# The 1e-9 of batch 0's softmax sums, added on GpSimd as separate pieces in a re-searched order

## The chip, the cores and the metric

The kernel runs on one core of a Trainium2 chip. The metric is the device time of one execution in microseconds (us), as the median of several runs; 699.75 us before the change (three runs, 699.62 to 700.32).

## The reference

Eight batches of slot attention with eight heads feed one feed-forward layer. Only what is computed matters here:

```python
a = np.exp(phi - np.max(phi, axis=2, keepdims=True))
a = a / (np.sum(a, axis=2, keepdims=True) + 1e-09)
k_m = np.einsum('bhsm,bhsd->bhmd', a, k)
v_m = np.einsum('bhsm,bhsd->bhmd', a, v)
scores = scale * np.matmul(q, k_m.transpose(0, 1, 3, 2))
attn = np.exp(scores - np.max(scores, axis=-1, keepdims=True))
attn = attn / (np.sum(attn, axis=-1, keepdims=True) + 1e-09)
attn_out = np.matmul(attn, v_m)
...
h = x @ w_in
g = 0.5 * h * (1.0 + erf(h * inv_sqrt2))
return g @ w_out
```

There are 576 positions per batch, 32 slots, heads of 64, a model width of 512 and a hidden width of 2048. x holds attn_out with the heads side by side. The 1e-9 that the title speaks of is the one in the second softmax, over the 32 slots.

## The kernel before, in words

The slot matrix v_m is multiplied into w_in (pieces `Up`, matmuls that write `pu`), so that hidden products run straight from the softmax weights: `h` = (p_hi, p_lo) times U. U and the weights p are each split into a high and a low part and go through three matmul passes; the same holds for g and w_out (`p`, 12 matmuls of 512 columns per block of 128 hidden units, with `gh`, `gl`, `wo_hi`, `wo_lo`). The weights arrive as 64-bit numbers and are decoded on the chip, one block of 128 hidden units at a time: two ScalarE instructions (`dB`, lines 309 and 310), three VectorE ones (`dC` 314, `dG` 318, `dS` 322) and an integer add on GpSimd (`dDi`, `dDo`, line 342); `dE` and `dF` split w_out. Sixteen such blocks exist for w_in and for w_out; the first eight serve batch 0 and batch 1 before the other eight are needed.

Batch 0 is treated apart, since nothing can run before its softmax. Its 576 positions are handled in three parts x = 0, 1, 2 (256, 256 and 64 positions). For each part the scores are transposed so that positions lie on partitions (`n_score`, writes `psc`), then VectorE takes the maximum (`n_max`, line 680) and subtracts it (`n_sub`, 685), ScalarE takes the exponential (`n_exp`, 692), VectorE sums over the slots (`n_sum`, 695), adds 1e-9 and takes the reciprocal (`n_inv`, 699 and 700), and multiplies (`n_mul`, also line 685). TensorE transposes back (`n_T`, writes `pT`, line 720), ScalarE and VectorE split the result into p_hi and p_lo (`n_hi` 735, `n_lo` 739). The sums are tiles `smx` of 128 partitions by 16, 16 and 8 numbers. The first hidden product (`h.0.0.0`, line 901) needs parts 0 and 1, the second half (`h.0.0.1`) needs parts 1 and 2.

All of this is written out as a list of some thousand pieces, `START`: a piece is a name with its arguments, as `n_inv.0` or `gelu.0.3.1`, and after a colon the engine where there is a choice (`a` ScalarE, `d` VectorE). `do` calls the function of each piece in the order of the list, and at the end every instruction is pinned behind the one before it on its engine. Each engine thus runs its own instructions in the list's order, and DMAs are issued from SyncE's queue in that order too. From batch 3 on, a plan by steps takes over where the list ends.

The hidden products alternate between two PSUM buffers (tag `h`, two of them): `h.0.1.1` writes the buffer that `gelu.0.0.1` (lines 921 and 922) has to have read. The pu products and the scores of later batches share one PSUM pair (tag `at`). One SBUF buffer serves phi of every batch, so phi of batch 1 is loaded once batch 0's transposes (line 457) have read it.

Of the kernel before, what the change touches and what calls it, by code (L numbers as in the profile page):

```python
# [64 lines left out]
at.1.1.4 at.1.0.4 dG.2.0 n_T.2 atc.1.1.4 atc.1.0.4:a n_hi.2 slots.1.0 dC.3.1 dDi.2 anorm.1
Lkv.1.1.3 n_lo.1 Lkv.1.1.4 n_lo.2 h.0.0.1 gelu.0.0.0 Lphi.2.0 dS.3.1 km.1.0 dG.3.1 Lwo.4
Up.0.2.1 gelu.0.0.1 Lwi.5 dF.2 dB.3.0 dDo.3 h.0.1.0 Lwo.7 Uh.0.2:d Lwo.5 Ul.0.2 h.0.1.1
gh.0.0:a Lphi.2.1 dC.3.0 Lwi.7 slots.1.1 gelu.0.1.1 gl.0.0 Lwi.6 gelu.0.1.0 dG.3.0 dE.3
h.0.2.0 km.1.1 dS.3.0 gh.0.1:a amax.2.0 dDi.3 dB.4.0 slotsT.1 h.0.2.1 kT.1:d dF.3 dB.4.1
Up.0.3.1 dC.4.0 dG.4.0 p.0.0 Uh.0.3 dB.5.0 gl.0.1 Ul.0.3 gelu.0.2.1 dG.5.0 gelu.0.2.0 dB.5.1  # L70
dC.4.1 dS.4.0 score.1.0 dC.5.0 dDi.4 h.0.3.0 Lq.1.1 sT.1.0.1 sT.1.0.0 Lwo.6 h.0.3.1 dS.5.0
dG.4.1 dDi.5 Up.0.4.1 gelu.0.3.1 max.1.0 p.0.1 Uh.0.4:a gelu.0.3.0 Ul.0.4 sub.1.0 dS.4.1
dC.5.1 exp.1.0 dDo.4 gh.0.2:a sum.1.0 Up.0.5.1 dG.5.1 h.0.4.0 Uh.0.5:a dE.4 gl.0.2 h.0.4.1
gh.0.3:a Ul.0.5 dS.5.1 p.0.2 dF.4 dDo.5 inv.1.0 gelu.0.4.1 amax.2.1 dB.6.0 dC.6.0 mul.1.0
gelu.0.4.0 dE.5 score.1.1 gl.0.3 dB.6.1 h.0.5.0 dS.6.0 dF.5 p.0.3 gh.0.4:a dG.6.0 dB.7.1
dC.6.1 dDi.6 pT.1.0 gelu.0.5.0 sT.1.1.1 dB.7.0 sT.1.1.0 dS.6.1 h.0.5.1 gl.0.4 dG.6.1 Up.0.6.1
gelu.0.5.1 gh.0.5:a dC.7.0 p.0.4 dDo.6 Uh.0.6 Ul.0.6 max.1.1 Lwi.9 sub.1.1 aexp.2.1 Lwo.8
Lwi.8 dG.7.0 exp.1.1 Up.1.0.4 Lwo.9 dC.7.1 dE.6:a gl.0.5 h.0.6.0 Uh.1.0 dS.7.0 p.0.5 dG.7.1
dDi.7 aexp.2.0 Ul.1.0 ph.1.0:a dS.7.1 dF.6 dDo.7 sum.1.1 gelu.0.6.0 Up.0.7.1 h.0.6.1 Uh.0.7:a
Ul.0.7 inv.1.1 h.0.7.0 gelu.0.6.1 dE.7:a gh.0.6:d h.0.7.1 gl.0.6 gelu.0.7.0 dB.8.1 p.0.6  # L80
pl.1.0 Lwo.10 dF.7 Lphi.3.1 gelu.0.7.1 Lwi.10 gh.0.7:a mul.1.1 dB.8.0 gl.0.7 dC.8.0 p.0.7
dB.9.0 pT.1.1 dG.8.1 dB.9.1 ph.1.1:d pl.1.1 o.0.2.7:a dC.9.0 h.1.0.0 dC.8.1 dS.9.0 h.1.0.1
dG.9.1 gelu.1.0.0 h.1.1.0 dC.9.1 gelu.1.0.1 dG.8.0 o.0.0.7:a h.1.1.1 dS.8.1 gh.1.0:a o.0.3.7:a
gl.1.0 Up.1.4.4 o.0.1.7:a dS.8.0 gelu.1.1.0 p.1.0 dG.9.0 dDi.8 gelu.1.1.1 Uh.1.4:a gh.1.1:a
Ul.1.4 dDo.8 h.1.2.0 dE.8:d Lwo.11 h.1.2.1 dF.8 Lq.2.0 gelu.1.2.0 Lwi.11 gl.1.1 h.1.3.0
gelu.1.2.1 gh.1.2:d h.1.3.1 gl.1.2 gelu.1.3.0 dB.10.1 p.1.1 Lwo.12 gelu.1.3.1 dG.10.1 dB.10.0
dC.10.1 dS.9.1 dC.10.0 dDo.9 dG.10.0 h.1.4.0 h.1.4.1 gelu.1.4.0 dDi.9 h.1.5.0 gelu.1.4.1
dE.9:a p.1.2 dF.9 Lwo.13 Lwi.13 gh.1.3:d dB.11.0 dS.10.1 Lwi.12 gl.1.3 dDo.10 gelu.1.5.0
gh.1.4:d h.1.5.1 dB.11.1 p.1.3 dE.10:d gelu.1.5.1 dS.10.0 amax.3.1 dDi.10 gl.1.4 h.1.6.0
dG.11.1 p.1.4 dC.11.1 gelu.1.6.0 gh.1.5:a gl.1.5 dF.10 dC.11.0 h.1.6.1 dS.11.0 dG.11.0 p.1.5  # L90
gelu.1.6.1 dS.11.1 dDi.11 dB.12.0 dB.12.1 dDo.11 h.1.7.0 dG.12.1 Lwi.14 dE.11:a mw.2 gh.1.6:a
Up.0.8.4 gl.1.6 h.1.7.1 Uh.0.8:a dF.11 p.1.6 dC.12.1 gelu.1.7.0 dG.12.0 gelu.1.7.1 gh.1.7:a
dS.12.1 dB.13.0 dDo.12 gl.1.7 p.1.7 dB.13.1 Ul.0.8 dC.12.0 dS.12.0 aexp.3.1 o.1.2.7:d dDi.12
h.0.8.0 dC.13.1 h.0.8.1 Lwi.15 gelu.0.8.0 dG.13.1 o.1.3.7:a Lphi.3.0 Up.1.8.4 gelu.0.8.1
dC.13.0 mr.2 o.1.1.7:d gh.0.8:a Lwo.15 h.0.9.0 o.1.0.7:d Lwo.14 h.0.9.1 dE.12:d gelu.0.9.0
dF.12 Uh.1.8:a h.0.10.0 dS.13.1 gl.0.8 dDo.13 p.0.8 Ul.1.8 dE.13:a gelu.0.9.1 dF.13 gh.0.9:a
h.0.10.1 dB.14.0 gl.0.9 p.0.9 dG.13.0 gelu.0.10.0 dS.13.0 gelu.0.10.1 gh.0.10:a dDi.13 gl.0.10
dB.15.0 h.0.11.0 dG.14.0 Up.0.12.2 dC.14.0 h.0.11.1 dC.15.0 Uh.0.12:a amax.3.0 dB.15.1 p.0.10
dG.15.0 mw.3 Lphin.2 dS.14.0 gelu.0.11.1 Ul.0.12 gelu.0.11.0 dDi.14 gh.0.11:a gl.0.11 h.0.12.0
dS.15.0 h.0.12.1 dDi.15 p.0.11 gelu.0.12.1 gelu.0.12.0 dB.14.1 gh.0.12:a Up.0.14.2 h.0.13.0  # L100
Uh.0.14:a Ul.0.14 h.0.13.1 gelu.0.13.0 gl.0.12 h.0.14.0 gelu.0.13.1 dG.14.1 gh.0.13:a p.0.12
dC.14.1 gelu.0.14.0 dS.14.1 dC.15.1 dDo.14 anorm.2 gl.0.13 aexp.3.0 Lphi.4.1 h.0.14.1 Lphi.4.0
dS.15.1 dG.15.1 Lkv.2.0.0 h.0.15.0 Lkv.2.0.2 dE.14:d dDo.15 p.0.13 gelu.0.15.0 gelu.0.14.1
gh.0.14:a gl.0.14 dF.14 h.0.15.1 dE.15:d p.0.14 gelu.0.15.1 gh.0.15:d dF.15 gl.0.15 aadd.2
p.0.15 o.0.0.15 mr.3 Lkv.2.1.0 o.0.1.15 Lkv.2.1.4 amax.4.0 Lkv.2.0.3 h.1.8.0 o.0.3.15 o.0.2.15
h.1.8.1 Lkv.3.0.2 gelu.1.8.0 Lkv.2.0.1 Up.1.12.4 gelu.1.8.1 Lkv.2.1.1 gh.1.8:a Lkv.2.1.2
h.1.9.0 Lkv.2.0.4 Uh.1.12:d Lkv.2.1.3 h.1.9.1 gelu.1.9.0 os.0.1 gl.1.8 h.1.10.0 Ul.1.12 p.1.8
gelu.1.10.0 gelu.1.9.1 gh.1.9:d gl.1.9 aexp.4.0 ax.2 h.1.10.1 p.1.9 gelu.1.10.1 slots.2.0
slots.2.1 h.1.11.0 km.2.1 Lphin.3 gh.1.10:d gl.1.10 h.1.11.1 gelu.1.11.0 Lkv.3.1.4 km.2.0
os.0.3 p.1.10 gelu.1.11.1 Lkv.3.0.4 gh.1.11 gl.1.11 slotsT.2 kT.2:d h.1.12.0 score.2.0  # L110
gelu.1.12.0 h.1.12.1 sT.2.0.0 Lq.2.1 aadd.3 Lkv.3.0.1 p.1.11 gelu.1.12.1 gh.1.12:a gl.1.12
sT.2.0.1 max.2.0 ax.3 p.1.12 h.1.13.0 h.1.13.1 gelu.1.13.0 h.1.14.0 gelu.1.13.1 gh.1.13:d
h.1.14.1 gelu.1.14.0 gl.1.13 p.1.13 gelu.1.14.1 gh.1.14:a gl.1.14 sub.2.0 exp.2.0 h.1.15.0
sum.2.0 h.1.15.1 inv.2.0 p.1.14 gelu.1.15.0 mul.2.0 gelu.1.15.1 gh.1.15:a pT.2.0 gl.1.15
tg.1.0 p.1.15 ph.2.0:d pl.2.0 o.1.0.15 Up.2.0.4 Lkv.3.1.0 Lq.3.1 tp.1.0 Uh.2.0:a Lkv.3.0.0
Ul.2.0 o.1.2.15 h.2.0.0 o.1.3.15 h.2.1.0 tg.1.1 score.2.1 gelu.2.1.0 o.1.1.15 gelu.2.0.0
tp.1.1 Lq.3.0 sT.2.1.0 sT.2.1.1 Lkv.3.1.1 max.2.1 Lkv.3.1.3 Lkv.3.0.3 amax.4.1 Lkv.3.1.2
tg.1.2 os.1.1 Up.2.12.4 anorm.3 Up.2.4.4 tg.1.3 tp.1.2 Uh.2.4:a Ul.2.4 aexp.4.1 h.2.2.0
Lphi.5.0 Up.2.8.4 Lphi.5.1 mw.4 h.2.3.0 Uh.2.8:d tp.1.3 gelu.2.3.0 gelu.2.2.0 gh.2.0.0:d
Ul.2.8 sub.2.1 gl.2.0.0 slots.3.0 to.1 gh.2.0.1:d slots.3.1 gl.2.0.1 Lkv.4.0.3 exp.2.1 os.1.3  # L120
h.2.4.0 sum.2.1 Lkv.4.0.2 P.2.0.0 mr.4 inv.2.1 Lphin.4 gelu.2.4.0 mul.2.1 Lkv.4.0.1 pT.2.1
Lkv.4.0.4 h.2.5.0 h.2.6.0 gelu.2.5.0 P.2.0.1 gelu.2.6.0 gh.2.0.2:a Uh.2.12:a gl.2.0.2 km.3.1
h.2.7.0 P.2.0.2 gelu.2.7.0 gh.2.0.3:d gl.2.0.3 Ul.2.12 P.2.0.3 km.3.0 amax.5.0 amax.5.1 mw.5
Lkv.4.1.1 h.2.8.0 Lkv.4.1.2 Lkv.4.1.0 h.2.9.0 Lkv.4.1.4 gelu.2.8.0 Lkv.4.1.3 slotsT.3
Lkv.4.0.0 kT.3 h.2.10.0 gelu.2.9.0 gh.2.0.4:d score.3.1 gelu.2.10.0 score.3.0 h.2.11.0
sT.3.0.1 sT.3.0.0 h.2.12.0 max.3.0 gelu.2.11.0 gh.2.0.5:a h.2.13.0 gl.2.0.4 gl.2.0.5
gelu.2.12.0 P.2.0.4 sT.3.1.1 aadd.4 sT.3.1.0 h.2.14.0 P.2.0.5 gelu.2.14.0 gelu.2.13.0 gh.2.0.6
ph.2.1:d max.3.1 aexp.5.0 anorm.4 h.2.15.0 gl.2.0.6 ax.4 sub.3.0 P.2.0.6 pl.2.1 gelu.2.15.0
# [1146 lines left out]
```

## Time and profile before

| | us |
|---|---|
| median of three runs | 699.75 |
| lowest, highest | 699.62, 700.32 |
| the profiled execution's own time | 699.25 |
| its span, first to last instruction | 697.5 |
| TensorE busy (matmul) | 683.4 |
| VectorE busy | 374.5 |
| ScalarE busy | 306.9 |
| GpSimd busy | 45.9 |

The profiled execution is 0.50 us under the median. A matmul's end is modelled, so TensorE's busy time is not its time at full rate; what can be read from it is where TensorE was idle, and for whom it waited. The mean granted TensorE clock was 0.991. "PEq", "SPq" and the like are sequencers, which issue and wait.

### The profile page before, as it was taken

What the parts mean: (1) busy time and instruction counts of PE and PEld (TensorE: products, weight loads), DVE (VectorE), ACT (ScalarE), POOL (GpSimd) and SP (SyncE); (2) the same over time, 40 slices, a digit from 0 to 9 for tenths busy, and PEclk for the clock granted to TensorE, in tenths of its full rate; (3) what the DMA queues carried; (4) which work ended last, traced back from release to release, by engine and by line L of the source; (5) the groups of instructions that cost most, each with busy time, mean ns of one, the idle gap of its engine ahead of it and who ended that gap; (6) DMA issues with size and microseconds to landing.
All of it is one profiled execution on the core that took longest, in us unless ns stands there. A gap on an engine that the chain in (4) does not pass through costs nothing.

```text
span 697.5 us, 12343 instructions
## 1 busy us (share of the span) xinstructions
PE 683.4 (98%) x4942; PEld 568.3 (81%) x4942; DVE 374.5 (54%) x691; ACT 306.9 (44%) x787; POOL 45.9 (7%) x38
## 2 busy tenths in 40 slices
...
GB/s 328 367 298 103 125 189 138 43 154 173 27 222 141 84 208 1 66 193 134 162 1 57 57 2 31 1 99 1 30 1 31 84 1 31 1 31 0 31 1 46
DMA packets 30717, 64.37 MB, mean 92 GB/s; under 512 B 3780, under 2 KB 8644, under 8 KB 30660
## 3 DMA queue, kind: packets, MB, share of 16 engines
...
q10 hardware_dynamic: 96, 0.13, 0.1%
q14 instruction: 18, 0.15, 0.1%
...
## 4 chain that ended last, share of the span: by engine, by line
PE 91%; DMA 3%; DVE 2%; ACT 1%; issue 0%; SPq 0%; POOL 0%; POOLq 0%; ACTq 0%; DVEq 0%
PE acc L941 49%; PE h L901 28%; PE tacc L941 6%; PE pu L619 4%; DMA kv<-kv 1%; PE psc L619 1%; DMA w_in_sb<-w_out 1%; PE psc L536 1%; DMA raw<-w_in 1%; DMA phi<-phiT 1%; PE x L536 1%; DVE raw L318 0%; PE pk L536 0%; DVE wo_lo L348 0%; ACT aT L244 0%
## 5 line engine op out<-in xcount | busy, mean ns | idle before, releaser
L901 PE MATMUL h<-p_hi,U 128*128 128x288 f32 x1024 | 203.2, 297 | 0.0
L941 PE MATMUL acc<-wo_hi,gh 128*128 128x512 f32 x512 | 200.4, 391 | 0.0
L941 PE MATMUL acc<-wo_hi,gl 128*128 128x512 f32 x512 | 199.6, 390 | 0.0
L941 PE MATMUL acc<-wo_lo,gh 128*128 128x512 f32 x512 | 199.6, 390 | 0.0
L913 ACT ACTIVATE gf<-h 128x256 f32<-128x256 f32 x192 | 74.0, 387 | 254.8 <-issue 180.0
L901 PEld LDWEIGHTS h<-p_hi,U 128*128 128x128 f32 x1024 | 163.5, 188 | 22.0 <-issue 7.9
L244 DVE CAST gh<-gf 128x512 fp32r<-128x512 f32 x103 | 44.2, 429 | 175.8 <-ACT gf L913 169.2
L941 PEld LDWEIGHTS acc<-wo_hi,gl 128*128 128x128 f32 x512 | 96.1, 188 | 21.1 <-DVE gl L928 0.6
L941 PEld LDWEIGHTS acc<-wo_hi,gh 128*128 128x128 f32 x512 | 96.4, 188 | 20.4 <-DVE gl L928 3.4
L941 PEld LDWEIGHTS acc<-wo_lo,gh 128*128 128x128 f32 x512 | 96.1, 188 | 15.8
L901 PE MATMUL h<-p_lo,U 128*128 128x288 f32 x512 | 108.7, 294 | 0.0
L928 DVE TENSOR_TENSOR gl<-gf,gh 128x512 fp32r<-128x512 f32 x128 | 90.4, 707 | 20.0 <-ACT gh L244 10.9
L901 PEld LDWEIGHTS h<-p_lo,U 128*128 128x128 f32 x512 | 81.2, 188 | 0.4 <-DVE p_lo L739 0.4
L860 DVE TENSOR_TENSOR U<-pu,U 128x512 fp32r<-128x512 f32 (+2 forms) x50 | 40.9, 836 | 44.0 <-ACT U L244 43.9
L244 ACT CAST U<-pu 128x512 fp32r<-128x512 f32 (+2 forms) x47 | 32.0, 710 | 18.3 <-PE pu L619 13.5
L915 ACT ACTIVATE tails<-h 128x32 f32<-128x32 f32 x192 | 37.3, 194 | 0.0
L619 PE MATMUL pu<-w_in_sb,kT 64*32 64x512 f32 (+2 forms) x624 | 34.4, 528 | 1.3 <-POOL w_in_sb L342 0.8
L941 PE MATMUL tacc<-wo_hi,gh_t 128*128 128x512 f32 x64 | 25.4, 397 | 0.0
L941 PE MATMUL tacc<-wo_lo,gh_t 128*128 128x512 f32 x64 | 24.9, 390 | 0.0
L941 PE MATMUL tacc<-wo_hi,gl_t 128*128 128x512 f32 x64 | 24.9, 390 | 0.0
L919 ACT ACTIVATE gf<-h 128x288 f32<-128x288 f32 x32 | 13.2, 414 | 24.6 <-PE h L901 15.9
L342 POOL TENSOR_TENSOR y<-y,raw 128x512 int32<-128x512 int32 x14 | 20.5, 1462 | 47.4 <-DVE y L322 23.6
...
## 6 DMA issues: line engine op xcount, KB each, us to landing
...
```

The source lines that it names most:

```text
L244: return e.copy(dst, src) if e is nc.scalar else e.tensor_copy(dst, src)
L342: nc.gpsimd.tensor_tensor(w, y, low, op=ALU.add)
L536: nc.tensor.matmul(pk[32 * j : 32 * j + 32, : 2 * D], st["aT", b][:, c, g, 32 * j : 32 * j + 32], st["kv", b, g, c][:, :, j, :], start=(c ...
L619: nc.tensor.matmul(ps[g][M * j : M * j + M], st["kT", b][rows, t, M * j : M * j + M], moving[j][rows], start=True, stop=True,)
L860: nc.vector.tensor_sub(u[:, ..., 1, :], pu, u[:, ..., 0, :].bitcast(F32))
L901: i = nc.tensor.matmul(h[:, :HS], u[g][w], x[:, g, :], start=(n == 0), stop=(n == 3 * G - 1))
L913: nc.scalar.activation(gf[:, f % 2 * n : f % 2 * n + n], h[:, :n], AF.Gelu)
L915: nc.scalar.activation(t, h[:, n:HS], AF.Gelu)
L919: nc.scalar.activation(gf[:, :HS], h[:, :HS], AF.Gelu)
L928: nc.vector.tensor_tensor(g_of("gl", *k), g_of("gf", *k), g_of("gh", *k).bitcast(F32), op=ALU.subtract)
L941: nc.tensor.matmul(acc, x, w[:, f, :], start=(first and n == 0), stop=(last and n == 2))
```

## The change

A piece `n_eps` holds the addition of 1e-9 for batch 0's parts, on GpSimd; `n_inv` keeps the reciprocal on VectorE. The order is a new one: the same 1004 pieces and the three `n_eps`, in a list that differs from its first line, with another choice of engine in 37 of the pieces. The other batches' addition (line 790 before) is not touched.

```diff
@@ -694,9 +694,12 @@
     def n_sum(x):
         nc.vector.tensor_reduce(part0(x, "smx"), part0(x, "s"), axis=AX.X, op=ALU.add)
 
+    def n_eps(x):
+        m = part0(x, "smx")
+        nc.gpsimd.tensor_scalar_add(m, m, 1e-9)
+
     def n_inv(x):
         m = part0(x, "smx")
-        nc.vector.tensor_scalar_add(m, m, 1e-9)
         nc.vector.reciprocal(m, m)
...
-        "n_inv": n_inv, "n_mul": n_mul, ...
+        "n_eps": n_eps, "n_inv": n_inv, "n_mul": n_mul, ...
@@ -50,99 +50,99 @@
 START = """
-Lwo.1 Lphi.0.1 Lphi.0.0 Lkv0.0.0 Lkv0.1.0 Lwo.0 dB.1.1 Lq.0.0 amax.0.1 Lq.0.1 dC.1.1 aexp.0.1
...
+Lwo.1 Lphi.0.1 Lphi.0.0 Lkv0.0.0 Lkv0.1.0 Lwo.0 dB.1.1 Lq.0.0 amax.0.1 aexp.0.1 amax.0.0
...
```

On VectorE, the place is the softmax of batch 0's parts 0 and 1. `smx` are the sums, `s` the exponentials, `mx` the maxima; line 348 is `dF`, line 860 (863 after) splits U, lines 314, 318 and 322 decode weights, line 426 is batch 1's maximum of phi. Before:

```order
L318 TENSOR_SCALAR raw_147<-raw_147 128x512
L695 TENSOR_REDUCE smx_0_376<-s_0_303 128x16
L426 TENSOR_REDUCE nm_280<-phi_209 128x1
L695 TENSOR_REDUCE smx_1_385<-s_1_339 128x16
L699 TENSOR_SCALAR smx_0_376<-smx_0_376 128x16
L700 RECIPROCAL smx_0_376<-smx_0_376 128x16
L680 TENSOR_REDUCE mx_2_399<-psc_2_305 128x8
L685 TENSOR_TENSOR s_0_303<-s_0_303,smx_0_376 128x512
L348 TENSOR_TENSOR wo_lo<-y_246,wo_hi 128x512
L860 TENSOR_TENSOR U_0_411<-pu_0_402,U_0_411 128x2x128
L699 TENSOR_SCALAR smx_1_385<-smx_1_385 128x16
L700 RECIPROCAL smx_1_385<-smx_1_385 128x16
```

and after:

```order
L695 TENSOR_REDUCE smx_0_350<-s_0_299 128x16
L322 TENSOR_SCALAR y_246<-y_246 128x512
L318 TENSOR_SCALAR raw_147<-raw_147 128x512
L426 TENSOR_REDUCE nm_271<-phi_185 128x1
L695 TENSOR_REDUCE smx_1_391<-s_1_346 128x16
L703 RECIPROCAL smx_0_350<-smx_0_350 128x16
L348 TENSOR_TENSOR wo_lo<-y_246,wo_hi 128x512
L685 TENSOR_TENSOR s_0_299<-s_0_299,smx_0_350 128x512
L863 TENSOR_TENSOR U_0_407<-pu_0_398,U_0_407 128x2x128
L703 RECIPROCAL smx_1_391<-smx_1_391 128x16
L314 TENSOR_SCALAR y_412<-y_412 128x512
L685 TENSOR_TENSOR s_1_346<-s_1_346,smx_1_391 128x512
```

The two additions are gone from VectorE, the first sum has moved ahead of two decoding steps, and the third part's maximum (line 680) has moved behind both multiplications.

On GpSimd, the place is the same stretch; after the change its queue reads:

```order
L342 TENSOR_TENSOR y_246<-y_246,raw_147 128x512
L342 TENSOR_TENSOR w_in_sb<-y_149,raw_134 128x4x128
L699 TENSOR_SCALAR smx_0_350<-smx_0_350 128x16
L342 TENSOR_TENSOR w_in_sb<-y_246,raw_147 128x4x128
L699 TENSOR_SCALAR smx_1_391<-smx_1_391 128x16
L342 TENSOR_TENSOR y_412<-y_412,raw_314 128x512
L699 TENSOR_SCALAR smx_2_482<-smx_2_482 128x8
L342 TENSOR_TENSOR w_in_sb<-y_412,raw_314 128x4x128
```

Before, the same line-342 additions stood there in the same order with nothing between them; now one of the three small additions stands behind each of three of them.

On ScalarE, the place is the first hidden products of batch 0; `gf` is the gelu's output, `h_0` and `h_1` the halves, `km` batch 1's slots, lines 309 and 310 a weight's decoding. Before:

```order
L919 ACT_TABLE_LOAD
L919 ACTIVATE gf_0_547<-h_0_0_478 128x288
L579 ACTIVATE km_552<-pk_0_506,rz_530 128x2x64
L921 ACTIVATE gf_0_547<-h_1_0_540 128x224
L922 ACTIVATE tails<-h_1_0_540 128x64
L309 ACTIVATE y_396<-w_in_sb 128x512
L310 ACTIVATE w_in_sb<-w_in_sb 128x512
```

and after:

```order
L922 ACT_TABLE_LOAD
L922 ACTIVATE gf_0_547<-h_0_0_474 128x288
L579 ACTIVATE km_551<-pk_0_508,rz_485 128x2x64
L309 ACTIVATE y_469<-w_in_sb 128x512
L310 ACTIVATE w_in_sb<-w_in_sb 128x512
L924 ACTIVATE gf_0_547<-h_1_0_540 128x224
L925 ACTIVATE tails<-h_1_0_540 128x64
```

A pair of decoding instructions has moved ahead of the gelu of the second half.

## Rows read from the trace of the kernel before

**Rows 1.** Windows by stage: from:to and length, then busy us by engine, clock, DMA.

```profile
core 0: us, PE busy (x) PEld busy (x) DVE busy (x) ACT busy (x) POOL busy (x), PEclk, DMA share, GB/s
...
15.00:35.00 20.00, 15.66 (x228) 10.79 (x229) 19.70 (x49) 16.92 (x41) 6.69 (x5) 0.74 0.98 369
35.00:62.00 27.00, 26.56 (x268) 20.00 (x267) 25.12 (x50) 24.25 (x53) 10.11 (x7) 1.00 0.53 193
62.00:693.00 631.00, 631.00 (x4338) 529.41 (x4336) 324.88 (x582) 257.61 (x678) 27.10 (x19) 1.00 0.23 74
```

**Rows 2.** The waits of TensorE: us in total, times, longest us.

```profile
PE pk L561 <- DMA kv<-kv: 1.8, 2, 1.6
PE pT L720 <- DVE s L685: 1.0, 3, 0.5
...
PE pu L619 <- DVE sT L758: 0.2, 1, 0.2
...
PE pu L619 <- DVE kT L244: 0.2, 1, 0.2
```

**Rows 3.** Timeline of VectorE, 23 to 32 us: start us, us, instruction.

```profile
23.90 0.65 DVE L699 TENSOR_SCALAR smx<-smx 128x16 f32<-128x16 f32 x1
24.58 0.25 DVE L700 RECIPROCAL smx<-smx 128x16 f32<-128x16 f32 x1
...
26.56 0.16 DVE L699 TENSOR_SCALAR smx<-smx 128x16 f32<-128x16 f32 x1
26.76 0.25 DVE L700 RECIPROCAL smx<-smx 128x16 f32<-128x16 f32 x1
...
30.96 0.34 DVE L699 TENSOR_SCALAR smx<-smx 128x8 f32<-128x8 f32 x1
31.34 0.20 DVE L700 RECIPROCAL smx<-smx 128x8 f32<-128x8 f32 x1
```

**Rows 4.** Timeline of GpSimd, 0 to 36 us; in brackets the idle time ahead.

```profile
1.01 0.29 POOL masks.py:199 TENSOR_SCALAR_AFFINE_SELECT ident<-ident 128x128 f32<-128x128 f32 x1
...
21.76 2.75 POOL L342 TENSOR_TENSOR w_in_sb<-y,raw 128x512 int32<-128x512 int32 x2 [4.32 <-DVE y L322]
29.97 1.30 POOL L342 TENSOR_TENSOR y<-y,raw 128x512 int32<-128x512 int32 x1 [5.46 <-ACT p_hi L735]
```

**Rows 5.** Timeline of TensorE, 19 to 62 us.

```profile
24.59 0.68 PE L619 MATMUL pu<-w_in_sb,kT 64*32 64x128 f32 x16 [0.82 <-POOL w_in_sb L342]
...
28.70 1.76 PE L457 MATMUL pt<-ident,phi 128*128 128x128 f32 x8
30.22 0.52 PE L901 MATMUL h<-p_hi,U 128*128 128x288 f32 x2
...
32.22 0.44 PE L720 MATMUL pT<-ident,s 128*128 128x128 f32 x2 [0.18 <-DVE s L685]
...
36.30 0.69 PE L901 MATMUL h<-p_hi,U 128*128 128x288 f32 x4
```

**Rows 6.** Timeline of ScalarE, 19 to 39 us.

```profile
29.44 0.68 ACT L735 CAST p_hi<-pT 128x288 fp32r<-128x288 f32 x2
...
35.65 0.22 ACT L922 ACTIVATE tails<-h 128x64 f32<-128x64 f32 x1
35.76 0.68 ACT L309 ACTIVATE y<-w_in_sb 128x512 f32<-128x512 f32 x1
...
36.90 0.60 ACT L244 CAST gh<-gf 128x512 fp32r<-128x512 f32 x1
```

**Rows 7.** Timeline of SyncE's DMA issues, 4 to 20 us: start us, us.

```profile
5.01 1.06 SPq L406 DMA_DIRECT2D q<-q  x2
10.64 0.33 SPq L358 DMA_DIRECT2D phi<-phiT  x1
```

**Rows 8.** Windows around the stretch of low TensorE clock, columns as in Rows 1.

```profile
20.00:30.00 10.00, 8.18 (x130) 5.90 (x122) 9.90 (x25) 8.31 (x20) 2.78 (x3) 0.50 1.04 387
30.00:40.00 10.00, 9.54 (x136) 7.21 (x135) 8.81 (x25) 9.12 (x25) 4.88 (x4) 0.99 0.87 318
```

More of the change, by code (lines that the diff above doesn't have):

```diff
@@ L65 @@
[L65 to L128, printed above, removed]
-gh.2.0.7 gl.2.0.7 h.2.0.1 slots.4.0 gelu.2.0.1 slots.4.1 h.2.1.1 Lphin.5 P.2.0.7 gelu.2.1.1
-Lkv.5.0.0 gh.2.1.0 Lkv.5.0.1 gl.2.1.0 Lkv.5.0.2 Lkv.5.0.3 km.4.0 km.4.1 Lkv.5.0.4 O.2.0.0
@@ new lines @@
+Uh.0.1:a dB.2.0 n_max.2 n_T.1 Ul.0.1 Lwi.5 dS.2.1 at.1.1.0 Lkv.1.1.2 n_sub.2 n_hi.0 at.1.0.0
+dG.2.1 n_exp.2 dB.3.1 n_lo.0 h.0.0.0 dDo.2 n_sum.2 anorm.1 atc.1.1.0 dC.2.0 n_eps.2
+atc.1.0.0:a n_inv.2 n_hi.1 n_mul.2 at.1.1.4 at.1.0.4 dG.2.0 n_T.2 atc.1.1.4 atc.1.0.4:a n_hi.2
+slots.1.0 dS.2.0 dC.3.1 Lkv.1.1.3 dDi.2 n_lo.2 n_lo.1 Lkv.1.1.4 h.0.0.1 gelu.0.0.0 Lwi.4
+dS.3.1 km.1.0 dB.3.0 Lwo.4 Up.0.2.1 dG.3.1 Lphi.2.0 h.0.1.0 Lwo.5 dC.3.0 gelu.0.0.1 dDo.3
+Uh.0.2:d Lphi.2.1 dE.2:a h.0.1.1 Ul.0.2 Lwo.6 gh.0.0:a dS.3.0 Lwi.6 slots.1.1 gelu.0.1.1 dF.2
@@ new lines @@
+Lwi.7 gelu.0.1.0 Lwo.7 dE.3 dG.3.0 h.0.2.0 km.1.1 gl.0.0 dB.4.0 dDi.3 slotsT.1 h.0.2.1 kT.1:d
+gh.0.1:a dF.3 gelu.0.2.0 Up.0.3.1 dC.4.0 p.0.0 Uh.0.3 dG.4.0 dB.5.0 gl.0.1 dC.5.0 gelu.0.2.1
+Ul.0.3 dS.4.0 dG.5.0 dDi.4 gh.0.2:a score.1.0 amax.2.0 dB.5.1 h.0.3.0 sT.1.0.0 Lq.1.1 sT.1.0.1
+dC.5.1 dB.4.1 h.0.3.1 gl.0.2 Up.0.4.1 dS.5.0 dC.4.1 dDi.5 p.0.1 Uh.0.4:a max.1.0 Ul.0.4
+sub.1.0 dG.4.1 exp.1.0 dS.4.1 p.0.2 sum.1.0 dDo.4 amax.2.1 gelu.0.3.0 gelu.0.3.1 dG.5.1 dE.4
+dS.5.1 gh.0.3:a dF.4 dDo.5 Up.0.5.1 dB.6.0 h.0.4.0 Uh.0.5:d Ul.0.5 h.0.4.1 inv.1.0 dE.5 Lwo.8
@@ new lines @@
+dC.6.0 gl.0.3 dB.6.1 score.1.1 dG.6.0 p.0.3 gelu.0.4.1 dC.6.1 dF.5 mul.1.0 dB.7.1 dS.6.0
+pT.1.0 dDi.6 gelu.0.4.0 h.0.5.0 sT.1.1.0 gh.0.4:a sT.1.1.1 dB.7.0 h.0.5.1 dS.6.1 gl.0.4
+Up.0.6.1 gelu.0.5.1 dG.6.1 p.0.4 Uh.0.6 dC.7.1 gelu.0.5.0 dDo.6 max.1.1 gh.0.5:a Ul.0.6 dG.7.1
+Lwi.9 Lwi.8 gl.0.5 aexp.2.0 Lq.2.0 Up.1.0.4 dC.7.0 aexp.2.1 dG.7.0 p.0.5 dE.6:a Lphi.3.0
+sub.1.1 Uh.1.0 dS.7.0 exp.1.1 dDi.7 Ul.1.0 dF.6 h.0.6.0 dS.7.1 Up.0.7.1 gelu.0.6.0 sum.1.1
+dDo.7 h.0.6.1 Uh.0.7:a Ul.0.7 inv.1.1 h.0.7.0 gelu.0.6.1 ph.1.0:a gh.0.6:d h.0.7.1 gl.0.6
```

102 lines of the change are left out of this document (75 added, 27 removed).

## The prediction, made before the result

> **What bounds the kernel now.** I read the shares of busy time first, then the span cut into stages, then what TensorE waited for, and only then the timelines of the 30 us in which the changed pieces stand. TensorE is busy 683.4 of 697.5 us (the table), but that is an average over unlike stages. Cut up [rows 1], it says more: from 62 to 693 us TensorE is busy for all 631.0 us, so nothing that VectorE or GpSimd does there can make the kernel shorter; it can only add a stall. The last 4.5 us are the final eviction and its DMA, which the change does not touch. What can be gained lies in the first 62 us, where TensorE is idle for 20.00 - 15.66 = 4.3 us from 15 to 35 and for 27.00 - 26.56 = 0.4 from 35 to 62; before 15 us no changed instruction stands.
>
> From 15 to 35 us VectorE is busy for 19.70 of 20 us, ScalarE for 16.92, and the DMA engines' share is 0.98 [rows 1]. This is the stage in which the three additions stand, and VectorE is the fullest engine in it. But the time comes out at TensorE, so the waits decide [rows 2]: it waited for VectorE's softmax multiplications 1.0 us in three pieces, for VectorE's two later releases 0.2 and 0.2, for key and value loads 1.8. Those on VectorE add up to 1.4 us, which caps what a lighter VectorE can give by itself.
>
> **The change part by part.** The sum is made against the profiled execution (699.25 us; its span is 697.5, and 1.75 lie around it). The median of the runs is 0.5 us above it, and I add that at the end.
>
> *Three additions leave VectorE.* From the start of each to the start of the reciprocal behind it [rows 3]: 24.58 - 23.90 = 0.68, 26.76 - 26.56 = 0.20, 31.34 - 30.96 = 0.38, together 1.26 us. They differ although they do nearly the same work. The first ends at 24.55, when GpSimd's pair of decoding additions ends (21.76 + 2.75 = 24.51); the third ends at 31.30, when another ends (29.97 + 1.30 = 31.27) [rows 3, 4]; the second, with GpSimd idle, takes 0.16. So two of them stood still until GpSimd was done. An addition that nothing holds costs 0.20, three cost 0.60. The bounds of what VectorE is freed of are 0.60 (the holding falls on whatever VectorE runs next) and 1.26 us. I take 1.26, since in the new order a sum or a reciprocal, and no addition, stands there, and the reciprocals took 0.25 and 0.20 with and without GpSimd running.
>
> The rule that speaks against this is in the Trainium skill, "SBUF — State Buffer", section "Who interferes with whom": VectorE's two-port and two-input instructions and GpSimd's share a port pair as an exclusive lock, the one that starts first keeps it, and the other blocks wholly. The two held additions agree with it. By the rule VectorE's decoding steps would inherit the holding, and the term would be 0.60 instead of 1.26.
>
> How much of the 1.26 us reaches TensorE? The first hidden product, at 30.22, does not wait for the softmax alone: ScalarE casts p_hi only at 29.44, and TensorE is still on eight transposes from 28.70 [rows 5, 6]. There I count nothing. Behind it stand the third part's wait of 0.18, at 32.22 [rows 5], and the two later releases of 0.2 and 0.2 [rows 2]; these go: -0.6 us. The bounds are 0, and the 1.26 that leave VectorE.
>
> *Three additions on GpSimd, with two handoffs each.* No trace shows an addition this small there. The nearest rows are a select over 128x128 at 0.29 and, as the other end, a decoding addition at 1.30 to 1.38 behind which it may stand [rows 4]. A handoff from GpSimd took 24.59 - 24.51 = 0.08 [rows 4, 5]. I take 0.29 + 2 x 0.08 = 0.45 us from sum to reciprocal. For part 0 the new order puts two decoding steps, a maximum and the next sum into that time, for part 1 a reciprocal, two tensor operations and the split of U: hidden. For part 2 only two tiny statistics and one decoding step (0.4 us) stand there, so the cost is 0 if GpSimd is free and up to 1.38 if it has just begun a decoding addition. I take 0. GpSimd itself has room: 6.69 us busy in these 20 [rows 1]. If the cover were gone, VectorE would stand at the reciprocal with all its decoding steps behind it, and the p split and TensorE behind those.
>
> *ScalarE's order at the first gelu.* Before, the second half's gelu was read out by 35.65 + 0.22 = 35.87, and the product that reuses its PSUM buffer came in the row at 36.30 [rows 5, 6], so there was some 0.7 us in hand (that row holds four matmuls in 0.69; the third is the one). Now a decoding pair stands ahead: 36.90 - 35.76 = 1.14 us [rows 6]. That is 1.14 - 0.7 = 0.4 us of TensorE waiting. It is bounded by 0 (ScalarE arrives earlier) and 1.14 (no slack at all). I take +0.4. The pu product that waited 0.2 for kT soon after takes part of it back, which I have already counted in the 0.6.
>
> *SyncE's queue.* The second piece of q (issued at about 5.5 us, the second of the two in its row) now stands behind batch 1's phi, which waits for its buffer until 10.64 [rows 7]. It leaves some 5.5 us later, and the loads behind it about one issue later (0.4). The scores that need it come after 16 us, so it is in time if it takes no more than the 5 us then left. The key and value load that ended TensorE's longest later wait (1.6 [rows 2]) may slip by 0.4, but behind it TensorE waited 0.82 more for GpSimd [rows 5], which covers that. Cost 0; the bounds are 0 and the 0.4.
>
> *The rest of the list.* TensorE has the same pieces, hidden products and projections are regrouped, ScalarE has one instruction more and VectorE four fewer. With TensorE full from 62 us on, none of that counts unless an input comes late. I take 0, with an upper end of one ScalarE decoding pair, 1.14.
>
> The sum: -0.6 + 0 + 0.4 + 0 + 0 = -0.2 us, 699.05 for the profiled execution, and with the 0.5 the runs' median lies above it, **699.5 us**. A change of 0.2% is 1.4 us, about what a measurement of this kernel can tell from no change, so this is "no change". The bounds of the terms give 699.75 - 1.26 = 698.5 and 699.75 + 1.14 = 700.9 as its own range.
>
> **The rivals.**
>
> *VectorE sets the whole start (chance 0.20).* If p_hi and the transposes at 28.70 come forward with VectorE, the full 1.26 us reaches TensorE, and the 0.4 of idle time between 35 and 62 us goes as well: 699.75 - 1.7 = 698.1. For it: VectorE's 19.70 of 20 us. Against it: at 29.44 ScalarE, and not VectorE, had the last word [rows 6].
>
> *GpSimd answers late (0.11).* Two of the three small additions find a decoding addition in front of them or running, and VectorE stands at the reciprocal for 1.3 us each: 699.75 + 2.6 - 0.6 = 701.8, slower. It decides once the answer takes longer than the work between sum and reciprocal, 0.4 us for part 2. For it: each stands right behind a decoding addition in GpSimd's queue. Against it: GpSimd is idle two thirds of the time. The same page of the skill would have the lock add to it, since a small addition that finds VectorE's instruction running also waits that one out.
>
> *ScalarE falls behind in the new order (0.08).* The pair ahead of the gelu is one of several such regroupings; two pairs that TensorE has to wait out in full are 2.3 us: 702.0 at most.
>
> *A second stretch of low clock (0.05).* The granted clock is 0.50 (1.2 GHz) from 20 to 30 us, after TensorE had been idle for much of the time before, and back at 2.4 GHz in the next ten, when TensorE is busy 9.54 of 10 us [rows 8]. Should TensorE idle more in the new order and the low clock last through those ten, half their work, some 4.8 us, would be added: 704.5.
>
> That the change does not do what it says is excluded by the order of instructions: the additions stand on GpSimd.
>
> **How the numbers follow.** No change has 0.56, faster by over 0.2% is the first rival, 0.20, and the other three make slower, 0.24. The range takes in the first rival down to 697.9 and the second and third up to 702.0, and leaves out the clock and what lies beyond either end of the others: from 697.9 to 702.0.
>
> **What would show it.** Right: VectorE's reciprocals start without idle time ahead, GpSimd's three additions last under 0.3 us, the wait of TensorE for the multiplication of part 2 is gone, a wait of some 0.4 us for the gelu of the first block appears near 36 us, and 62 to 693 us is as full as before. Wrong: idle time ahead of a reciprocal with GpSimd as its releaser; the first hidden product more than 1 us off 30.22; or TensorE idle behind 62 us.

## The result, and the profile after

| | before | after |
|---|---|---|
| median, us | 700.03 | 703.4 |
| lowest, highest, us | 699.01, 700.63 | 701.89, 703.53 |
| the profiled execution's own time, us | 699.25 | 701.89 |
| its span, us | 697.5 | 700.1 |
| time to the first block of second-layer products, us | 41.47 | 41.59 |
| from that block to the end, us | 656.0 | 658.5 |

The change is slower: ratio 1.0051, 95% interval 1.0038 to 1.0063, some 3.4 us. (One of the six executions after the change took 1729.08 us; it is left out.) The forecast was 699.5, with a range up to 702.0.

The last two lines of the table cut the span at the first matmul that writes `acc`. The first part holds waits for loads, up to 3.3 us of them for keys and values, and differed by 2 us between traces of kernels with the same start. The second part hardly differs between traces of one order: three traces of the new order gave 658.5, 658.6 and 658.6 us. So 2.5 us of the loss lie behind 41 us, where the forecast had expected nothing. Windows by stage after the change (columns as in Rows 1):

```profile
core 0: us, PE busy (x) PEld busy (x) DVE busy (x) ACT busy (x) POOL busy (x), PEclk, DMA share, GB/s
15.00:35.00 20.00, 16.03 (x211) 11.52 (x212) 18.30 (x44) 15.71 (x38) 8.51 (x8) 0.66 0.98 367
35.00:62.00 27.00, 26.57 (x268) 20.08 (x268) 25.46 (x52) 23.39 (x51) 9.71 (x7) 1.00 0.58 213
...
100.00:150.00 50.00, 48.95 (x311) 40.15 (x310) 40.03 (x64) 32.87 (x70) 14.75 (x11) 1.00 0.22 77
150.00:200.00 50.00, 50.00 (x364) 40.90 (x363) 26.88 (x50) 18.61 (x37) 0.00 (x0) 1.00 0.37 100
```

Against [rows 1], VectorE has 1.4 us less to do between 15 and 35 us, with five instructions fewer, three of them the additions, and by 41 us TensorE stands where it stood. But TensorE, which was busy for all of 62 to 693 us [rows 1], now stands idle for 1.05 us between 100 and 150. What it waited for, after the change:

```profile
engine line waited for: us in total, times, longest us
...
PE pu L619 <- POOL w_in_sb L342: 1.6, 1, 1.6
PE psc L661 <- ACT sc L244: 1.1, 2, 0.6
PE h L904 <- ACT gf L922: 1.0, 1, 1.0
PE pu L619 <- DVE U L863: 1.0, 1, 1.0
...
PE psc L619 <- PE h L904: 0.4, 1, 0.4
```

The wait for the softmax multiplications and VectorE's two releases [rows 2] are gone, as forecast. A wait of 1.0 us for a gelu is new. Idle time of TensorE is not the whole account, since a matmul can also run long without the trace calling it a wait. So I compare when the same block of second-layer products begins in the two traces (`p.b.f` is batch b, hidden block f; the last row is the first block of batch 2's second half):

| block | before | after | later by | gained since the row above |
|---|---|---|---|---|
| p.0.0 | 41.47 | 41.59 | 0.12 | |
| p.0.7 | 74.58 | 75.18 | 0.60 | 0.48 |
| p.1.7 | 111.63 | 112.19 | 0.56 | -0.04 |
| p.0.15 | 148.92 | 150.87 | 1.94 | 1.38 |
| p.1.15 | 188.24 | 190.47 | 2.23 | 0.29 |
| batch 2 | 251.46 | 254.13 | 2.67 | 0.44 |

Behind 254 us the delay stays within 0.05 us to the end. The lost time has addresses, and the largest is between p.1.7 and p.0.15. There the timeline of ScalarE after the change reads:

```profile
start us, us, engine line op out<-in xcount [idle before <-releaser]
...
135.34 1.28 ACT L509 ACT_TABLE_LOAD   x1
136.64 1.17 ACT L509 ACTIVATE aT<-aT 128x1152 f32<-128x1152 f32 x1
...
138.72 0.78 ACT L432 ACTIVATE phi<-phi,nm 128x576 f32<-128x576 f32 x1
139.40 0.19 ACT L432 ACTIVATION_READ_ACCUMULATOR phi<-phi,nm 128x1 f32 x1
141.96 1.28 ACT L922 ACT_TABLE_LOAD   x1 [2.37 <-PE h L904]
143.25 0.41 ACT L922 ACTIVATE gf<-h 128x288 f32<-128x288 f32 x1
```

and that of TensorE:

```profile
142.23 0.43 PE L904 MATMUL h<-p_hi,U 128*128 128x288 f32 x2
143.71 0.53 PE L904 MATMUL h<-p_hi,U 128*128 128x288 f32 x2 [1.05 <-ACT gf L922]
144.08 0.42 PE L904 MATMUL h<-p_lo,U 128*128 128x288 f32 x2
144.34 0.43 PE L904 MATMUL h<-p_hi,U 128*128 128x288 f32 x2
144.61 0.40 PE L944 MATMUL acc<-wo_hi,gh 128*128 128x512 f32 x1
```

The new order puts two exponentials of later batches (pieces `ax.2` and `aexp.3.1`) ahead of `gelu.0.14.0`. The gelu's table must come back behind them, and it comes only at 141.96, when the gelu's input is there, although ScalarE had been idle for 2.37 us. Three hidden products stand in a row in TensorE's order (h.0.14.0, h.0.14.1, h.0.15.0). The third writes the PSUM buffer that `gelu.0.14.0` has yet to read, so TensorE waits for the load. Before, a table load of the same length stood in the same stretch:

```profile
141.54 1.28 ACT L919 ACT_TABLE_LOAD   x1 [0.28 <-DVE gl L928]
142.88 0.41 ACT L919 ACTIVATE gf<-h 128x288 f32<-128x288 f32 x1
```

but it ran ahead of its gelu's input, beside the last hidden product, and a block of p came next on TensorE:

```profile
142.41 0.43 PE L901 MATMUL h<-p_hi,U 128*128 128x288 f32 x2
142.68 0.39 PE L941 MATMUL acc<-wo_hi,gh 128*128 128x512 f32 x1
```

The next hidden product, which needed the buffer that these gelus read, stood behind that block, at 145.40, and did not wait.

The Trainium skill, "ScalarE: Activation LUTs", section "What ACT_TABLE_LOAD costs", gives 1.28 us for the load and 2.66 for the whole switch, with a drain. The trace agrees with the load; the gelu follows it by 0.01 us, and no drain is seen here.

### The profile page after: what moved, and what is told of

Read it like the earlier page. It is cut to its first block, busy times and chain, and to the rows that moved or that the text cites. A ratio compares the mean times of both kernels' runs of the same rounds, so it can differ in the third digit from the quotient of the medians.

```text
span 700.1 us, 12356 instructions
## 1 busy us (share of the span) xinstructions
PE 685.2 (98%) x4942; PEld 569.2 (81%) x4942; DVE 380.5 (54%) x687; ACT 309.1 (44%) x788; POOL 47.4 (7%) x41
## 4 chain that ended last, share of the span: by engine, by line
PE 96%; DVE 1%; ACT 1%; DMA 1%; issue 0%; SPq 0%; ACTq 0%
PE acc L944 50%; PE h L904 30%; PE tacc L944 6%; PE pu L619 5%; PE psc L619 1%; PE psc L536 1%; PE pk L561 1%; DMA phi<-phiT 1%; PE pt L457 1%; PE x L536 1%; PE psc L661 0%; PE pT L723 0%; PE pk L536 0%; DVE raw L318 0%; ACT L922 0%
## 5 line engine op out<-in xcount | busy, mean ns | idle before, releaser
L342 POOL TENSOR_TENSOR w_in_sb<-y,raw 128x512 int32<-128x512 int32 x14 | 19.6, 1404 | 35.3 <-DVE y L322 11.9
```

The lines of the kernel that those rows point to most:

```text
L342: nc.gpsimd.tensor_tensor(w, y, low, op=ALU.add)
```

## The experiments

My theory was that the place of the additions costs nothing and the new order costs everything. The rivals were the additions on GpSimd, and the start alone. Each kernel is described by its edit (an order is new or old up to a piece, which the table gives by its time); "C" is the time from the first block of second-layer products to the end of the span, in its own trace.

| kernel | C, us | median, us | ratio to before (95%) |
|---|---|---|---|
| before | 656.0 | 699.0 to 700.0 | |
| change, again | 658.6 | 702.01 | 1.0043 (1.0031, 1.0056) |
| new order, additions on VectorE | 658.6 | 702.84 | 1.0053 (1.0040, 1.0067) |
| old order, additions on GpSimd | 655.8 | 699.21 | 1.0000 (0.9990, 1.0009) |
| change + early gelu table | 657.3 | 702.26 | 1.0044 (1.0031, 1.0056) |
| the same, again | 657.3 | 701.42 | 1.0032 (1.0023, 1.0042) |
| new to 75 us, then old | 656.5 | 700.33 | 1.0016 (1.0007, 1.0025) |
| old, new from 75 to 149 us, old | 659.1 | 701.80 | 1.0035 (1.0024, 1.0046) |
| old to 149 us, then new | 658.0 | 701.82 | 1.0038 (1.0025, 1.0051) |
| change, two exponentials moved | 658.5 | 702.21 | 1.0040 (1.0027, 1.0052) |
| change, three repairs | 657.6 | 701.39 | 1.0031 (1.0019, 1.0043) |
| three repairs, q early | 657.4 | 701.07 | 1.0029 (1.0019, 1.0039) |
| old to 75 us, then new with two repairs | 656.4 | 699.36 | 1.0001 (0.9992, 1.0011) |
| change, early table, kT moved, U on ScalarE | 658.6 | 702.34 | 1.0043 (1.0030, 1.0055) |
| new to 30 us, then old | 656.6 | 700.39 | 1.0015 (1.0005, 1.0024) |
| old, new from 30 to 41 us, old | 656.2 | 700.43 | 1.0013 (1.0004, 1.0021) |
| new to 41 us, then old | 657.6 | 701.51 | 1.0038 (1.0026, 1.0051) |

### Place against order

The change unaltered:

> The changed kernel once more, for its spread and a second trace. Theory A (the new order's stalls behind 47 us, above all one of 1.2 us at 142 us where a table load stands in front of a gelu) expects 2.6 to 3.5 us over the kernel before and the same 1.2 us at the same place. Theory B (the GpSimd additions cost it) expects the same total, but with TensorE's loss inside the first 47 us.

The new order, with the additions put back on VectorE:

```diff
     def n_eps(x):
         m = part0(x, "smx")
-        nc.gpsimd.tensor_scalar_add(m, m, 1e-9)
+        nc.vector.tensor_scalar_add(m, m, 1e-9)
```

> The new order with the three additions back on VectorE, at the places where the pieces stand. Theory A: as slow as the changed kernel, 2.5 to 3.5 us over the kernel before, with the stall at 142 us. Theory B: within 0.7 us of the kernel before.

The order of before, with `n_eps.x` on GpSimd right behind each `n_sum.x`:

> The order of before, with the three additions on GpSimd, each right behind its sum in the list. Theory A: within 0.7 us of the kernel before, since TensorE sees nothing of them after 47 us. Theory B: 2 to 3.5 us slower than the kernel before.

The three answer at once. The order with the additions back on VectorE is as slow as the change (1.0053, and the same C); the old order with the additions on GpSimd is as fast as before (1.0000), which excludes a cost of the additions of more than 0.7 us. In that kernel GpSimd's queue reads:

```profile
start us, us, engine line op out<-in xcount [idle before <-releaser]
23.00 1.50 POOL L342 TENSOR_TENSOR w_in_sb<-y,raw 128x512 int32<-128x512 int32 x1 [5.87 <-DMA kv<-kv]
24.58 0.26 POOL L699 TENSOR_SCALAR smx<-smx 128x16 f32<-128x16 f32 x1
24.92 1.28 POOL L342 TENSOR_TENSOR w_in_sb<-y,raw 128x512 int32<-128x512 int32 x1
26.29 0.58 POOL L699 TENSOR_SCALAR smx<-smx 128x16 f32<-128x16 f32 x1
...
32.49 0.24 POOL L699 TENSOR_SCALAR smx<-smx 128x8 f32<-128x8 f32 x1
```

and the third reciprocal did stand still for GpSimd there:

```profile
32.76 0.20 DVE L703 RECIPROCAL smx<-smx 128x8 f32<-128x8 f32 x1 [0.58 <-POOL smx L699]
```

So the wait that the second rival feared exists in that order, at 0.58 us, but C is 0.2 us shorter than before and the time shows no loss.

### The table load

The change, with a gelu on a tiny tile behind `aexp.3.1`, which brings the table back early:

```diff
+    def gelu_table():
+        nc.scalar.activation(warm_exp, warm_exp, AF.Gelu)
...
-... p.0.12 Uh.0.14:a aexp.3.1 Ul.0.14 ...
+... p.0.12 Uh.0.14:a aexp.3.1 wg Ul.0.14 ...
```

> The changed kernel with one gelu of 8 numbers behind the last exponential ahead of 142 us, so that the gelu table is loaded before TensorE's product is ready. Theory A: 1.0 to 1.3 us faster than the changed kernel, and the wait of 1.0 us of a hidden product for a gelu is gone. Theory B: no difference from the changed kernel.

ScalarE's timeline there:

```profile
140.96 0.19 ACT L432 ACTIVATION_READ_ACCUMULATOR phi<-phi,nm 128x1 f32 x1
141.15 1.28 ACT L1036 ACT_TABLE_LOAD   x1
142.45 0.21 ACT L1036 ACTIVATE warm_exp<-warm_exp 128x8 f32<-128x8 f32 x1
143.53 0.41 ACT L922 ACTIVATE gf<-h 128x288 f32<-128x288 f32 x1 [0.87 <-PE h L904]
```

The load now runs in ScalarE's idle time, TensorE's wait is gone, and C falls from 658.6 to 657.3. The time hardly fell with it: in the profiled execution TensorE waited 3.3 us for key and value loads and the first block began at 43.13. Taken again:

> The change with an early load of the gelu table, once more. Theory: from the first block of second-layer products to the end it takes 1.1 us less than the change (657.4 against 658.5), and the whole is 0.5 to 1.5 us under the change's 702.0 to 703.4, since the late key and value loads of the first look were that execution's own. Rival (something that the early load itself brings about makes the front late by as much as it saves): again 702.0 to 702.5, with that first block 1 us or more later than in the change.

C was 657.3 again and the first block began at 41.48. Over both runs the mean of 15 executions is 701.70 against 702.51 in ten of the change: 0.8 us (95% interval 0.2 to 1.5), where C shows 1.2. The load is real, and is about a third of the loss.

Another cure, which would save a pair of loads: both exponentials moved down to `aexp.3.0`, behind `gelu.0.15.0` (line numbers of kernels with a shorter list are two lower):

```diff
-... gl.0.12 ax.2 dG.15.1 ... Uh.0.14:a aexp.3.1 Ul.0.14 ... dF.14 aexp.3.0 ...
+... gl.0.12 dG.15.1 ... Uh.0.14:a Ul.0.14 ... dF.14 ax.2 aexp.3.1 aexp.3.0 ...
```

> The change, with the two exponentials ax.2 and aexp.3.1 moved behind gelu.0.14.0, right ahead of aexp.3.0, so that one pair of table loads goes and gelu.0.14.0 finds its table in place. Theory: TensorE's wait of 1.0 us for that gelu is gone and the time is 1.0 to 1.4 us under the change's. Rival (what is late then waits elsewhere, as the first try with an early load could be read): the wait is gone and the time is within 0.3 of the change's, with a new wait behind 143 us.

The rival was right. ScalarE now does two loads and three exponentials in one piece, in front of the next gelu:

```profile
144.65 1.28 ACT L507 ACT_TABLE_LOAD   x1
145.94 1.17 ACT L507 ACTIVATE aT<-aT 128x1152 f32<-128x1152 f32 x1
147.01 0.76 ACT L430 ACTIVATE phi<-phi,nm 128x576 f32<-128x576 f32 x1
...
147.77 0.76 ACT L430 ACTIVATE phi<-phi,nm 128x576 f32<-128x576 f32 x1
...
148.65 1.28 ACT L922 ACT_TABLE_LOAD   x1
149.94 0.36 ACT L922 ACTIVATE gf<-h 128x224 f32<-128x224 f32 x1
```

The wait at 143 us is gone, and instead TensorE waits 0.6 us ahead of p.0.15, at 151 us, for the g that this gelu feeds; C stays at 658.5.

### Mixed orders

Two lists can be spliced: one up to a piece, then the other without what has been done. The new order up to p.0.7:

> The new order up to p.0.7 (75 us), with its additions on GpSimd, and the old order behind it. Theory (the loss is spread along the new order, most of it in the late part): 0.3 to 0.7 us above before, since the trace of the change had lost 0.60 us at that piece; TensorE does not wait for a gelu near 142 us. Rival (the loss is the front's: the regrouped stretch from 47 to 75 us and what it leaves behind): 2 to 3 us above before. Rival (the additions on GpSimd): 2 us or more here, and nothing in the two other mixes' difference.

The new order from p.0.7 to p.0.15 alone:

> The old order up to p.0.7 (75 us), the new one to p.0.15 (149 us), the old one behind. Theory: 1.3 to 1.6 us above before, of which 1.0 to 1.2 at 142 us, where TensorE waits for a gelu behind an exposed table load. Rival (front): 0 to 0.3 above before. Rival (the table load is caught up with later, since it stands ahead of a stretch that waits anyway): 0 to 0.3 above before, with the wait in the trace all the same.

The new order behind p.0.15 alone:

> The old order up to p.0.15 (149 us), the new one behind. Theory: 0.5 to 0.9 us above before, lost between 150 and 254 us in several small waits, constant from there on. Rival (front or table load alone): 0 to 0.2 above before.

All three came out above what the theory expected. The losses add up to 6.2 us (ratios 1.0016, 1.0035, 1.0038 on 699.0), twice the whole. The joints cost: the middle kernel has the 1.0 us at the table load, and behind its second joint, at 158 us, a wait that neither order has:

```profile
engine line waited for: us in total, times, longest us
PE acc L942 <- DVE gl L929: 1.7, 1, 1.7
```

The third kernel has a gelu wait of 1.0 us at 153 us, again from a misplaced table load. So these sums of parts are no account; only the first is read at face value: by p.0.7 it is 0.46 us late, as the change is, and 0.3 of that is left at the last block.

### Repairs

Three repairs in the change: the early table; `p.0.2` back behind `h.0.4.1`, since `score.1.1` waits there for a PSUM buffer (0.38 at 55.66 us in the change); and `slotsT.3 kT.3` behind `gelu.2.8.0`, since ScalarE's copy of kT stands before a gelu that TensorE needs at 231 us:

```diff
-... dS.4.1 p.0.2 sum.1.0 ... Ul.0.5 h.0.4.1 inv.1.0 ... score.1.1 ...
+... dS.4.1 sum.1.0 ... Ul.0.5 h.0.4.1 p.0.2 inv.1.0 ... score.1.1 ...
-... h.2.8.0 slotsT.3 kT.3 Lkv.4.1.3 h.2.9.0 gelu.2.8.0 ...
+... h.2.8.0 Lkv.4.1.3 h.2.9.0 gelu.2.8.0 slotsT.3 kT.3 ...
```

> The change with the early gelu table, with p.0.2 behind h.0.4.1 again (so that score.1.1 does not wait for the PSUM pair), and with slotsT.3 and kT.3 behind gelu.2.8.0. Theory (the loss is these three stalls in the order): from the first block of second-layer products to the end 656.2 to 656.8 us, as before's 656.0, and in all 699.5 to 700.7. Rival (the stalls only move): 657.4 or more from that block, 702 in all.

The third repair works: between p.1.15 and batch 2 the loss is 0.13 in place of 0.44. The second fails: from p.0.0 to p.0.7 the loss grows from 0.48 to 1.13 us. Without p.0.2 in front, TensorE meets another table load:

```profile
52.43 0.54 PE L902 MATMUL h<-p_hi,U 128*128 128x288 f32 x2 [1.52 <-ACT gf L920]
```

p.0.2 had been that load's cover: in the change it starts at 50.25, and the load at 50.36. A different cure for the same wait leaves p.0.2 and gives `Uh.0.5` to ScalarE, as before:

```diff
-... h.0.4.0 Uh.0.5:d Ul.0.5 h.0.4.1 ...
+... h.0.4.0 Uh.0.5:a Ul.0.5 h.0.4.1 ...
```

> The change with the early gelu table, slotsT.3 and kT.3 moved, and Uh.0.5 on ScalarE as before, with p.0.2 left where the change has it. Theory (score.1.1 waits for the split of U that stands on VectorE behind an instruction held 1.8 us): the wait of 0.4 us at 55 us goes, and from the first block of second-layer products to the end 656.5 to 656.9 us instead of the change's 658.5. Rival (the PSUM pair is late whoever splits U): 657.0 to 657.2.

Worse again: C is 658.6 with the other two repairs in, and TensorE waits 2.0 us at 55 us. The reason stands on VectorE in the change itself:

```profile
52.97 1.80 DVE L348 TENSOR_TENSOR wo_lo<-y,wo_hi 128x512 fp32r<-128x512 f32 x1
54.69 0.41 DVE L244 CAST U<-pu 128x256 fp32r<-128x256 f32 x1
55.14 0.42 DVE L863 TENSOR_TENSOR U<-pu,U 128x256 fp32r<-128x256 f32 x1
```

beside this on GpSimd:

```profile
52.92 1.30 POOL L342 TENSOR_TENSOR y<-y,raw 128x512 int32<-128x512 int32 x1 [0.94 <-DVE y L322]
```

and this on ScalarE, the next decoding pair:

```profile
54.81 0.67 ACT L309 ACTIVATE y<-raw 128x512 f32<-128x512 f32 x1 [1.35 <-DVE wo_lo L348]
```

A subtraction that takes 0.68 elsewhere (at 57.65) lasts until 0.55 us after GpSimd's addition ends at 54.22, as if it had stood still until then. The decoding pair writes a buffer `y` and waits for that subtraction, and with the split of U on ScalarE it stands behind the pair: 56.06 instead of 54.69. So the wait goes back to the held subtraction, whoever splits U; no run moved the addition on GpSimd away from it.

Last, the three repairs with q's second piece loaded as early as before:

> The three repairs, and q's second piece loaded ahead of batch 1's phi as before. Theory: like the three repairs within 0.5 us. Rival (the moved load makes the new front late): 0.6 to 1.2 us less than the three repairs, with the first block of second-layer products as much earlier.

and the old order up to p.0.7 with the new one behind it, early table and kT repair in:

> The old order up to p.0.7 (75 us), behind it the new one with the early gelu table and slotsT.3 and kT.3 moved. Theory: the old front and a rest without the new stalls, within 0.5 us of before. Rival (the rest of the new order has stalls that the trace does not name): 1 us or more above before.

The early q changes nothing that can be told (1.0029 against 1.0031). The last kernel is as fast as before, 1.0001. So behind 75 us the table load and the place of kT are most of what the new order loses. Its C is still 0.4 above before's: 0.3 of that is lost between p.0.15 and p.1.15, as in the change, and the trace shows no wait for it.

### The start

What is left is the start, and one trace of it decides little. Each execution's time less 1.78 us (what lies around the span) and less its kernel's C is when the first block began in it, if C does not change from one execution to the next. For the new start (ten measurements, 70 executions) the mean is 42.20 us; for the old start with the additions on GpSimd (four, 34 executions) 41.52; for before (five, 89) 41.60. Taken execution by execution the new start is later by 0.68 us, 95% interval 0.34 to 1.02. That interval is too narrow, since kernels with the same start differ by more: the four old ones give 40.89, 41.34, 41.82 and 42.14. Taken kernel by kernel the difference is 0.66, interval -0.16 to 1.48, and 0.53 against before, 0.13 to 0.93. The traces' own first blocks, 42.03 us on average over the eleven with the whole new start and 41.93 over the five with the old, show nothing. So a later start is likely and its size is open; the place of the additions makes no difference that can be told (42.26 in the new order with them on VectorE). Where in the start?

> The new order up to the first hidden product (30 us), the old one behind. From that block to the end 655.8 to 656.4 us by every theory. Theory (the new front is late because TensorE waits more before 30 us, and its clock falls again): the mean of the times is 0.5 to 0.9 us above before's. Rival (the front is lost between 30 and 41 us, or only by the scatter of the loads): within 0.3 of before.

> The old order up to the first hidden product, the new one from there to the first block of second-layer products (41 us), the old one behind. Theory (lost before 30 us): within 0.3 us of before. Rival (lost between 30 and 41 us): 0.5 to 0.9 above.

> The new order up to the first block of second-layer products (41 us), the old one behind. Theory (the new front costs by itself): the mean of the times 0.5 to 0.9 us above before's. Rival (the fronts are equal, and what the sums leave is scatter): within 0.3 of before.

The times are 1.1, 0.9 and 2.4 us above before's on average, the last far above what was expected, and C of the first is 656.6, above the 656.4 that every theory allowed. By the same reckoning the first block came at 42.15, 42.35 and 42.50, against 41.67 for before in the same rounds: each half comes out late by itself, against both theories, and the first of them within the noise (0.5, interval -0.2 to 1.2). The third is the least certain: of its C, 0.7 us is a last store that ended late in that one trace, so its first block may lie that much later; 0.8 is lost between p.0.0 and p.0.7, where the joint is. As joints cost elsewhere, this doesn't place the loss.

What the traces do show is two waits that come with the new list. In all twelve whose list is new up to the first hidden product, TensorE waits 0.51 and 0.59 us for ScalarE's copies `sc`, at 15 to 20 us, and 0.9 to 1.1 for the split of U, at 26 to 28. In the other six the first is at most 0.23 and the second is absent, but TensorE waits 0.6 to 1.0 for the softmax multiplications instead. No run took these waits out, so the start stays open.

## Why the prediction was wrong

**The step that failed** is "The rest of the list": cost 0, since "with TensorE full from 62 us on, none of that counts unless an input comes late", with an upper end of 1.14. Inputs do come late: behind the first block the list loses 2.5 us, of which 1.2 to 1.4 is one table load, 0.5 lies between 47 and 75 us, and 0.7 behind 150 (0.3 of it the place of kT). The sign that the prediction named as wrong, TensorE idle behind 62 us, is there. I had priced a regrouped ScalarE by its decoding pairs and not by its table loads, which the order of instructions shows without any time. The third rival had the mechanism (ScalarE late for the hidden products), with 0.08 and a top of 702.0. The start, later by some 0.5 to 0.7 us if the reckoning holds, was in no term: "before 15 us no changed instruction stands" misread a list that differs from its first line, and TensorE's new waits for `sc` begin at 15.1.

**VectorE's relief, bounds 0.60 to 1.26, 1.26 taken.** The reciprocals run at 0.24, 0.23 and 0.20 without idle time ahead of them, as forecast. But a decoding addition on GpSimd ran from 29.84 to 31.15, and this stood beside it:

```profile
30.48 0.70 DVE L439 TENSOR_SCALAR sm<-sm 128x2 f32<-128x2 f32 x1
```

An addition over 128x18 takes 0.17 when GpSimd is idle (at 55.48 us), so some 0.5 us of the holding went to another small instruction, and the relief was nearer the lower bound. The Trainium skill's rule, weighed in the prediction ("SBUF — State Buffer", section "Who interferes with whom"), says so; the trace agrees.

**TensorE's 0.6.** The three waits went, and others came in their place: 1.6 for GpSimd in place of 0.82 [rows 5], 1.0 for the split of U. So the 0.6 did not come. The first hidden product began at 30.48 in place of 30.22, the first block 0.12 later.

**GpSimd's additions, 0.29 each.** In the change:

```profile
22.69 0.94 POOL L699 TENSOR_SCALAR smx<-smx 128x16 f32<-128x16 f32 x1
23.72 1.28 POOL L342 TENSOR_TENSOR w_in_sb<-y,raw 128x512 int32<-128x512 int32 x1
25.09 0.58 POOL L699 TENSOR_SCALAR smx<-smx 128x16 f32<-128x16 f32 x1
...
31.24 0.51 POOL L699 TENSOR_SCALAR smx<-smx 128x8 f32<-128x8 f32 x1
```

The "under 0.3" is right for a free one (0.24 and 0.26 in the old order) and wrong here: the first ends at 23.63, when VectorE's 16-bit mask ends at 23.58, the second at 25.67, behind a two-input subtraction that ended at 25.56, and the third at 31.75, behind a decoding step that ended at 31.71. The cost of 0 was right, by the kernel with the old order. The second rival fell with it: no reciprocal waited in the change, and where one did, the time showed no loss.

**ScalarE's pair at the first gelu, +0.4.** The row that answers to 36.30 [rows 5] has four matmuls in 0.92 in place of 0.69, so 0.23 us: right in place, half in size.

**SyncE's queue, 0.** Not refuted: loading q early gave nothing.

**The other rivals.** VectorE did not set the start: the first hidden product did not come forward. A second stretch of low clock, given 0.05, did come, though not as the rival had it. In the change's trace the granted clock is 0.50 (1.2 GHz) from 16 to 22 us, 1.00 (2.4 GHz) from 23 to 25, where TensorE is busy 0.33 of 2 us, and 0.50 again from 26 to 32; before, it was 1.00 from 10 to 20 and 0.50 from 20 to 30 [rows 8]. From 30 to 40 it is 0.89, so it did not last through those ten. What it costs is not shown: of the traces with the new list up to the first hidden product, the one with the lowest mean clock from 10 to 42 us (0.71) has its first block at 41.38, and one with the highest (0.89) at 43.49.
